# Later head pairs of a sink-and-window attention: two score blocks merged into 128 columns before the softmax, one transpose per head and block, and a triangle mask that parts them again

## The chip, the cores and the metric

The kernel runs on one core of one Trainium2 chip. The metric is device time in microseconds (us) of one execution; the kernel before takes 735.0 us as the median of three runs (734.63 to 736.55). The five engines of the core each work through their own instruction queue in order: PE (matrix multiply, with its weight loads shown apart as PEld), DVE (VectorE), ACT (ScalarE), POOL (GpSimd) and SP (which here only issues transfers). They meet through semaphores.

## The reference

The input has 4 batches, 8 heads, 768 positions and head width 64. Each query sees the first 4 keys (the sinks) and the 128 keys that end with its own position. The attention output then goes through a two-layer network of widths 512, 2048 and 512.

```
scores = scale * np.matmul(q, k.transpose(0, 1, 3, 2))
rel = pos[:, None] - pos[None, :]
keep = (pos[None, :] < n_sink) | ((rel >= 0) & (rel < window))     # n_sink = 4, window = 128
scores = np.where(keep, scores, -1e9)
a = softmax(scores); x = matmul(a, v)       # then per token, over all heads:
h = x @ w_in;  g = h * np.tanh(softplus(h));  out = g @ w_out
```

With a window of 128, a query at row r of a 128-row block sees of its own block the columns c <= r, and of the block before it the columns c > r. Of any column number, it sees one of the two.

## The kernel before, in words

**Tiling.** Work is cut into 12 chunks of 256 tokens (T = 256, two blocks of P = 128 rows; `TB = 2`). Each batch gives three chunks, c3 = 0, 1, 2. A chunk needs four head pairs of attention (`pair`, line 364) and eight steps of the two-layer network (`step`, line 468). The four chunks with c3 = 0 come first; their pairs are the "first" ones (16 pairs). The other eight chunks have the "later" pairs (32 pairs), and only these are touched by the change. The network steps of chunks 3 to 10 are "wide": the first layer uses one 512-column and one 256-column product per weight tile (lines 493 and 494), and DVE adds the halves (line 503).

**A later pair.** A query block needs three groups of key columns: the 128 keys of the older block, 32 sink columns (SK = 32), and the 128 keys of its own block. They lie side by side in `ks`, 288 columns in all (W2). For each of the two blocks and each of the two heads:

- PE makes 288 scores per query into a PSUM tile `st` (line 399).
- DVE adds the mask `m2`, scales, and finds the row's extreme in one pass (line 407, from `st` into `p2`).
- ACT takes the exponential with the row sum (line 410). Two short operations give the reciprocal (lines 413 to 415).
- ACT or DVE multiplies the row by it (lines 420 and 421).
- PE transposes two squares of 128 columns, the older and the own one (line 431), into a PSUM tile `pt`; ACT or DVE copies `pt` to `pth` in SBUF (line 435, by the helper at lines 256 and 259).

Then, once per pair, the 32 sink columns of both blocks and heads are gathered in `psk` (line 439), transposed together (line 440) and copied to `sks`. `out` (line 446) multiplies `pth` by the values (line 449, twelve products) and adds the sink part (line 453, four). The result is split into a high and a low part for the network (lines 457 and 458).

**Order of the work.** A planner (`Plan.solve`, line 123) simulates the engines with fixed costs for every task and gives each engine a fixed order. Each task has a rank (pairs run some nine to eleven steps ahead of the network steps that need them, `att_rank`, line 585) and one or several ways, that is engines which can do it with their planned costs; the planner takes whichever can start first, ties by rank. Tasks on POOL, and those DVE tasks that are marked `shared`, are planned one after the other and never at once. Buffers have a fixed number of places (`TAGS`, line 233): four PSUM places named `att` for scores, transposes and attention outputs, two `p2`, one `pth`. Where the plan leaves PE without work for more than 250 ns, `emit` (line 590) puts in filler products on zeros (line 622).

The costs that the planner uses for what the change touches:

```
def dve_t(n, fast=False): return ((n / 2 if fast else n) + 66) / 0.96      # ns
def pool_t(n): return 149 + 2.1 * n
a = add(r + OTP, {PE: (109 * (2 if cols[0] is None else 4), tr)}, norm, [p2], [pt])
```

**Masks.** `constants` (line 780) builds the masks once at the start on DVE. `body` (line 814) tests whether the window is at most 129 and sinks at most 32; if so the fast form runs, else a general one.

Of the kernel before, what the change touches and what calls it, by code (L numbers as in the profile page):

```python
# [12 lines left out]
F32 = mybir.dt.float32  # L13
BF16 = mybir.dt.bfloat16
F32R = mybir.dt.float32r
I32 = mybir.dt.int32
U32 = mybir.dt.uint32
AF = mybir.ActivationFunctionType
ALU = mybir.AluOpType
# [4 lines left out]
P = 128  # L24
NBLK = S // P
SK = 32
PITCH = P + SK
# [4 lines left out]
TB = 2  # L32
T = TB * P
NCH = NBLK // TB
BIG = 3.0e38
# [7 lines left out]
LAG = {PE: {PE: 0, ACT: 200, DVE: 200}, ACT: {PE: 270, ACT: 143, DVE: 142, POOL: 170}, DVE: {PE: 200, ACT: 120, DVE: 127, POOL: 155},  # L43
       POOL: {PE: 203, ACT: 75, DVE: 80, POOL: 102}, SP: {}}
W2 = 2 * P + SK
PEN_C, PEN_S, PEN_N, PEN_J = 200, 0, 0, 0
OTP, OVP = 1.2, 1
WA, WB, WO = 1.5, -5, 1.5
# [18 lines left out]
def dve_t(n, fast=False):  # L67
    return ((n / 2 if fast else n) + 66) / 0.96
# [161 lines left out]
class Fast(Base):  # L230
# [16 lines left out]

    def setup(self):
        c = self.c
        self.m0, self.m1, self.m2 = c.m0, c.m1, c.m2  # L250

    def copy_ways(self, n, dst, src, psum=False, engines=(ACT, DVE), scale=None):
        nc = self.nc
# [110 lines left out]
    def pair(self, b, c3, pr, rank, x, x_done):  # L364


        nc, add = self.nc, self.plan.add
        first = c3 == 0
        (ks, qh, vt, ldk, ldv), vr, vdeps = self.operands(b, c3, pr, rank - 3)
        pth = Buf("pth", [P, 2, 2 * T])  # L370
        if not first:
            ssk, sks = Buf("att", [P, P]), Buf("sks", [P, P])
        p2 = Buf("p2", [P, TB, 2, W2])
        last, norms = [], []
        for i in range(TB):
            r = rank + i
            nm, sm, rc = Buf("nm", [P, 2]), Buf("sm", [P, 2]), Buf("rc", [P, 2])
            if not first:
                n, mask, c0 = W2, self.m2, i * PITCH
            elif i == 0:  # L380
                n, mask, c0 = P, self.m0, 0
            else:
                n, mask, c0 = 2 * P, self.m1, 0
            st = [Buf("att", [P, n]) for _ in range(2)]

            def mov(rows, n=n, c0=c0):
                if n == 2 * P:
                    return ks.t[rows, 0:2 * PITCH].rearrange("p (a c) -> p a c", c=PITCH)[:, :, 0:P]
                return ks.t[rows, c0:c0 + n]

            def qk(st=st, mov=mov, i=i, c0=c0, n=n):
                cols = slice(i * P, (i + 1) * P)
                for e in range(2):
                    rows = slice(e * D, (e + 1) * D)
                    if first:
                        yield nc.tensor.matmul(st[e].t, qh.t[rows, cols], mov(rows), start=True, stop=True)  # L396
                    else:
                        for n_, part in enumerate(qh):
                            yield nc.tensor.matmul(st[e].t, part.t[:, e, cols], ks[e].t[:, c0:c0 + n], start=n_ == 0, stop=n_ == 1)  # L399
            cost = 2 * (n / 1.2 + 106) + 100 if first else pe_t(*[n] * 4)  # L400
            s = add(r, {PE: (cost, qk)}, ldk, [ks, qh] if first else [*ks, *qh], st)
            ex = []
            for e in range(2):
                new = ([p2] if i == 0 else []) + [nm, sm] if e == 0 else []
                old = [z for z in (p2, nm, sm) if z not in new]
                pv = lambda e=e, n=n, i=i: p2.t[:, i, e, 0:n]
                a = add(r + .03 + .01 * e, {DVE: (dve_t(n) + 8, lambda st=st, pv=pv, nm=nm, e=e, mask=mask, n=n: nc.vector.tensor_tensor_reduce(  # L407
                    out=pv(), in0=st[e].t[:, 0:n], in1=mask, scale=-0.125, scalar=BIG, op0=ALU.add, op1=ALU.min, accum_out=nm.t[:, e:e + 1]))},
                    [s], [st[e]] + old, new)
                a = add(r + .05 + .01 * e, {ACT: (act_t(n, ptr=2), lambda pv=pv, nm=nm, sm=sm, e=e: nc.scalar.activation(  # L410
                    pv(), pv(), AF.Exp, bias=nm.t[:, e:e + 1], scale=-1.0, accum_out=sm.t[:, e:e + 1]))}, [a], [p2, nm, sm])
                ex.append(a)
            a = add(r + .07, {ACT: (act_t(2), lambda rc=rc, sm=sm: nc.scalar.activation(rc.t, sm.t, AF.Copy, bias=1e-9), 0, PEN_N),
                              DVE: (72, lambda rc=rc, sm=sm: nc.vector.tensor_scalar(rc.t, sm.t, 1e-9, None, ALU.add))}, ex, [sm], [rc])
            a = add(r + .08, {DVE: (84, lambda rc=rc: nc.vector.reciprocal(rc.t, rc.t))}, [a], [rc])
            norm = []
            for e in range(2):
                row = lambda e=e, n=n, i=i: p2.t[:, i, e, 0:n]
                norm.append(add(r + .09 + .01 * e, {
                    DVE: shared((dve_t(n, True) + 80, lambda row=row, rc=rc, e=e: nc.vector.tensor_scalar(row(), row(), rc.t[:, e:e + 1], None, ALU.mult))),  # L420
                    ACT: (act_t(n, ptr=1), lambda row=row, rc=rc, e=e: nc.scalar.activation(row(), row(), AF.Copy, scale=rc.t[:, e:e + 1]), 0, PEN_N),  # L421
                }, [a], [p2, rc]))
            norms += norm
            pt = Buf("att", [P, 2, T])
            cols = (0, PITCH) if not first else ((None, 0) if i == 0 else (0, P))

            def tr(pt=pt, cols=cols, i=i):
                for e in range(2):
                    for x in range(2):
                        if cols[x] is not None:  # L430
                            yield nc.tensor.transpose(pt.t[:, e, x * P:(x + 1) * P], p2.t[:, i, e, cols[x]:cols[x] + P], self.ident)  # L431
            a = add(r + OTP, {PE: (109 * (2 if cols[0] is None else 4), tr)}, norm, [p2], [pt])
            lo = P if cols[0] is None else 0
            dst = slice(i * T + lo, (i + 1) * T)
            last.append(add(r + OTP + .05, self.copy_ways(2 * (T - lo), lambda dst=dst: pth.t[:, :, dst], lambda pt=pt, lo=lo: pt.t[:, :, lo:], True),
                            [a], [pt] + ([] if i == 0 else [pth]), [pth] if i == 0 else []))
        if not first:
            psk = Buf("psk", [P, 2 * TB, SK])
            a = add(rank + 1.11, self.copy_ways(P, lambda: psk.t, lambda: p2.t.rearrange("p i e c -> p (i e) c")[:, :, P:PITCH]), norms, [p2], [psk])
            a = add(rank + OTP + 1.02, {PE: (109, lambda: nc.tensor.transpose(ssk.t, psk.t.rearrange("p a c -> p (a c)"), self.ident))}, [a], [psk], [ssk])  # L440
            last.append(add(rank + OTP + 1.09, self.copy_ways(P, lambda: sks.t, lambda: ssk.t, True), [a], [ssk], [sks]))
        r = rank + TB + OVP
        o = Buf("att", [P, T])
        jobs = self.jobs(first)

        def out():
            for n_, (j, c0, c1, o0, o1) in enumerate(jobs):
                for e in range(2):
                    yield nc.tensor.matmul(o.t[e * D:(e + 1) * D, o0:o1], vt.t[:, e, j, :], pth.t[:, e, c0:c1],  # L449
                                           start=n_ == 0, stop=first and n_ == len(jobs) - 1)  # L450
            if not first:
                for i in range(TB):
                    yield nc.tensor.matmul(o.t[:, i * P:(i + 1) * P], vr.t[:, i, :], sks.t, start=False, stop=i == TB - 1)  # L453
        cost = sum(c1 - c0 for _, c0, c1, _, _ in jobs) / .6 + 200 + (0 if first else T / .6 + 50)
        a = add(r + .05, {PE: (cost, out)}, last + ldv + vdeps, [pth, vt] + ([] if first else [vr, sks]), [o])
        h = x[pr]
        a = add(r + .15, self.copy_ways(T, lambda: h.t[:, 0, :], lambda: o.t, True), [a], [o], [h])
        c = add(r + .17, self.sub_ways(T, lambda: h.t[:, 1, :], lambda: o.t, lambda: f32(h.t[:, 0, :]), (DVE,)), [a], [o, h])
        x_done += [a, c]
# [320 lines left out]
def constants(nc, top, tmp, lim):  # L780
# [14 lines left out]
    nc.vector.tensor_scalar(ahead, rel, 0.0, 1.0e6, ALU.is_lt, ALU.mult)  # L795
    nc.vector.tensor_tensor(rel, rel, ahead, ALU.max)
    c.done = nc.vector.tensor_copy(col, col_i)
    c.m0, c.m1, c.m2 = t([P, P], F32, "m0"), t([P, 2 * P], F32, "m1"), t([P, W2], F32, "m2")

    def masks():  # L800
        nsink, window = lim[:, 0:1], lim[:, 1:2]
# [1 line left out]
        drop(col, col, nsink)  # L803
        drop(c.m1[:, P:], rel[:, P:], window)
        nc.vector.tensor_tensor(c.m0, c.m1[:, P:], col, ALU.max)
        drop(c.m2[:, 0:P], rel[:, 0:P], window)
        nc.vector.tensor_tensor(c.m1[:, 0:P], c.m2[:, 0:P], col, ALU.max)
        nc.vector.tensor_copy(c.m2[:, P:PITCH], col[:, 0:SK])
        nc.vector.tensor_copy(c.m2[:, PITCH:], c.m1[:, P:])
    c.masks = masks  # L810
    return c

# [1 line left out]
def body(tc, q, k, v, vs, w_in, w_out, limits, out):  # L814
    nc = tc.nc
    with ExitStack() as ctx:
# [17 lines left out]
        with ExitStack() as c2:  # L834
# [14 lines left out]
            nsink_f, window_f = lim[:, 0:1], lim[:, 1:2]  # L849
            nc.vector.tensor_scalar(ok, nsink_f, float(SK), None, ALU.is_le)  # L850
            nc.vector.scalar_tensor_tensor(ok, window_f, 1.0, ok, ALU.is_ge, ALU.mult)
            nc.vector.scalar_tensor_tensor(flag, window_f, P + 1.0, ok, ALU.is_le, ALU.mult)
            c.masks()
        banded = nc.values_load(flag[0:1, 0:1], min_val=0, max_val=1)
        with tc.If(banded > 0) as cmp:
# [43 lines left out]
```

## Time and profile before

| what | number |
|---|---|
| median of three runs | 735.0 us (734.63 to 736.55) |
| span of the profiled execution, first to last instruction | 732.8 us |
| what lies around that span, if the execution was like the median | 2.2 us |
| PE busy | 717.3 us, 98% |
| DVE busy | 543.9 us, 74% |
| ACT busy | 569.8 us, 78% |
| POOL busy | 134.0 us, 18% |
| later pairs: first score product to last sink product | 194.8 to 668.2 us |

The profiled execution's own time is known by its span alone. Busy shares are unions of overlapping instructions. PE's products are pipelined: a product of 128 columns is listed with some 270 ns, but the next one begins long before it ends, so what a product costs PE is the distance from its start to the start of the next. A line of the timeline gives the start, the duration of the merged instructions, the engine, the line of the kernel, the operation, the tiles as out<-in, the shape and the count; in brackets stands the idle time before it and what ended it. A line of the groups gives the summed busy time, the mean of one instruction in ns, and the idle time before.

### The profile page before, as it was taken

The numbers are of one execution on the slowest core, as the hardware profiler recorded it, in microseconds if no ns is written. First come the engines' busy times: TensorE is split into PE (matmuls) and PEld (weight loads), VectorE is DVE, ScalarE is ACT, GpSimd is POOL, SyncE is SP. The second block draws the span as 40 slices with busy tenths as digits, with TensorE's granted clock in tenths as the row PEclk, the third lists the DMA queues.
The fourth block names the chain that finished last, engine by engine and source line by source line (L and its number), as shares of the span: only waits on it lengthen the run. The fifth ranks groups of instructions, "written<-read, shape, count | busy, mean of one in ns | idle before, by whom it ended". The sixth has DMA issues, their size and how long they took to land.

```text
span 732.8 us, 12975 instructions
## 1 busy us (share of the span) xinstructions
PE 717.3 (98%) x4468; PEld 605.3 (83%) x4468; DVE 543.9 (74%) x1419; ACT 569.8 (78%) x1288; POOL 134.0 (18%) x109
## 2 busy tenths in 40 slices
PE   6999999999999999999999999999999999999996
PEld 4667889888888888888888888888888888888995
DVE  5999999996778877768877667777777867664432
ACT  5999989777977788787788878787787788775653
POOL 0232231201120222121012121130132223100000
PEclk9999999999999999999999999999999999999999
DMA  6555433423353323323233323223313311100000
GB/s 212 163 172 166 139 103 133 124 86 90 103 138 93 82 75 89 81 74 98 65 92 93 79 65 102 72 64 111 87 45 95 109 31 34 49 17 2 30 1 33
DMA packets 48987, 64.12 MB, mean 87 GB/s; under 512 B 4880, under 2 KB 41744, under 8 KB 48912
## 3 DMA queue, kind: packets, MB, share of 16 engines
q1 hardware_dynamic: 48480, 61.62, 29.0%
q10 hardware_dynamic: 432, 1.57, 0.6%
q8 instruction: 37, 0.61, 0.4%
q14 instruction: 38, 0.31, 0.1%
HBM read 56.89 MB, written 6.29 MB: 86 GB/s over the span
## 4 chain that ended last, share of the span: by engine, by line
PE 90%; DVE 4%; ACT 4%; DMA 1%; issue 1%; SPq 0%; ACTq 0%; DVEq 0%
PE acc L527 35%; PE hp L493 16%; PE hp L497 10%; PE hp L494 8%; PE att L449 5%; PE att L399 4%; PE att L431 4%; PE att L453 3%; PE att L497 2%; ACT p L410 1%; PE att L396 1%; DMA qh<-q_p 1%; ACT p L421 1%; DVE p L407 1%; ACT w L256 1%; DVE w L305 1%
## 5 line engine op out<-in xcount | busy, mean ns | idle before, releaser
L527 PE MATMUL acc<-w,gh 128*128 128x512 f32 x768 | 198.4, 396 | 0.2 <-ACT gh L256 0.2
L493 PE MATMUL hp<-w,w 128*128 128x512 f32 x512 | 192.1, 409 | 0.0
L527 PEld LDWEIGHTS acc<-w,gh 128*128 128x128 f32 x768 | 136.1, 188 | 26.3 <-ACT gh L256 0.8
L494 PE MATMUL hp<-w,w 128*128 128x256 f32 x512 | 143.3, 280 | 0.0
L503 DVE TENSOR_REDUCE n<-hp 128x256 f32<-128x512 f32 x128 | 87.8, 687 | 30.5 <-PE hp L494 29.6
L493 PEld LDWEIGHTS hp<-w,w 128*128 128x128 f32 x512 | 96.3, 188 | 17.1 <-issue 0.2
L527 PE MATMUL acc<-w,gl 128*128 128x512 f32 x384 | 108.3, 390 | 0.0
L410 ACT ACTIVATE p<-p,nm 128x288 f32<-128x288 f32 (+1 forms) x192 | 95.3, 499 | 3.6 <-DVE nm L407 3.5
L494 PEld LDWEIGHTS hp<-w,w 128*128 128x128 f32 x512 | 96.8, 189 | 1.5
L407 DVE CUSTOM_DVE_ANT_0 p<-att,m 128x288 f32<-128x288 f32 (+1 forms) x192 | 74.6, 419 | 25.2 <-PE att L399 20.2
L508 ACT ACTIVATE u<-u,bias 128x512 f32<-128x512 f32 x96 | 69.0, 720 | 29.8 <-DVE u L507 29.8
L497 PE MATMUL hp<-w,w 128*128 128x256 f32 x672 | 89.6, 285 | 0.2 <-DVE n L511 0.2
L497 PEld LDWEIGHTS hp<-w,w 128*128 128x128 f32 x672 | 84.9, 191 | 3.9 <-issue 0.5
L527 PEld LDWEIGHTS acc<-w,gl 128*128 128x128 f32 x384 | 71.9, 188 | 14.1
L506 ACT ACTIVATE u<-n 128x512 f32<-128x512 f32 x64 | 40.5, 632 | 54.1 <-DVE n L503 54.1
L267 POOL TENSOR_TENSOR gl<-n,gh 128x512 fp32r<-128x512 f32 x32 | 41.4, 1293 | 202.6 <-ACT gh L256 173.1
L256 ACT ACTIVATE gh<-n 128x512 fp32r<-128x512 f32 x93 | 58.3, 626 | 20.4 <-DVE n L511 20.3
L507 DVE TENSOR_SCALAR u<-u 128x512 f32<-128x512 f32 x96 | 44.7, 466 | 38.2 <-ACT u L506 37.6
L509 ACT ACTIVATE u<-u,bias 128x512 f32<-128x512 f32 x96 | 68.9, 718 | 1.7
L511 DVE SCALAR_TENSOR_TENSOR n<-u,n 128x512 f32<-128x512 f32 x64 | 44.1, 690 | 35.1 <-ACT u L510 34.9
L510 ACT ACTIVATE u<-u 128x512 f32<-128x512 f32 x96 | 60.1, 627 | 1.8
L269 DVE TENSOR_TENSOR gl<-n,gh 128x512 fp32r<-128x512 f32 x64 | 48.2, 754 | 15.4 <-PE acc L527 12.2
(85 smaller groups left out, 1063.3 us busy)
## 6 DMA issues: line engine op xcount, KB each, us to landing
raw<-k_p SPq DMA_DIRECT2D x64, 224.0 KB, 3.5
w<-q_p SPq DMA_DIRECT2D x64, 128.0 KB, 3.2
raw<-w_out SPq DMA_DIRECT2D x15, 512.0 KB, 4.0
raw<-w_in SPq DMA_DIRECT2D x14, 512.0 KB, 3.5
y<-u SPq DMA_DIRECT2D x24, 256.0 KB, 2.0
vt<-v_b SPq DMA_DIRECT2D x32, 192.0 KB, 2.5
vsr<-v_s SPq DMA_DIRECT2D x32, 128.0 KB, 2.3
ks<-k_p SPq DMA_DIRECT2D x16, 144.0 KB, 3.4
```

Source lines behind the costliest of these rows:

```text
L256: ways[ACT] = act_t(n, psum), lambda: nc.scalar.activation(dst(), src(), AF.Copy, scale=scale or 1.0)
L269: way = dve_t(n), lambda: nc.vector.tensor_tensor(dst(), a(), b(), ALU.subtract)
L407: a = add(r + .03 + .01 * e, {DVE: (dve_t(n) + 8, lambda st=st, pv=pv, nm=nm, e=e, mask=mask, n=n: nc.vector.tensor_tensor_reduce(out=pv() ...
L410: a = add(r + .05 + .01 * e, {ACT: (act_t(n, ptr=2), lambda pv=pv, nm=nm, sm=sm, e=e: nc.scalar.activation(pv(), pv(), AF.Exp, bias=nm.t[: ...
L493: yield nc.tensor.matmul(hp.t, wih[f].t[:, fs], xt, start=kt == 0, stop=False)
L494: yield nc.tensor.matmul(hp.t[:, 0, :], wil[f].t[:, fs], xt[:, 0, :], start=False, stop=kt == KT - 1)
L497: yield nc.tensor.matmul(hp.t[:, y, :], w_.t[:, fs], xt[:, z, :], start=kt == 0 and n_ == 0, stop=kt == KT - 1 and n_ == 2)
L503: hs.append(add(r + .3 + .1 * y, {DVE: (dve_t(2 * T), lambda y=y, hp=hp: nc.vector.tensor_reduce(m.t[:, y, :], hp.t.rearrange("p z t -> p ...
L508: a = add(r + .52, {ACT: (act_t(N, ptr=1), lambda: nc.scalar.activation(u.t, u.t, AF.Square, bias=self.one))}, [a], [u])
L509: a = add(r + .53, {ACT: (act_t(N, ptr=1), lambda: nc.scalar.activation(u.t, u.t, AF.Ln, bias=self.half, scale=0.5))}, [a], [u])
L510: a = add(r + .54, {ACT: (act_t(N), lambda: nc.scalar.activation(u.t, u.t, AF.Exp, scale=-1.0))}, [a], [u])
L527: yield nc.tensor.matmul(acc[t].t, g_.t[:, y, ts_], w_.t, start=new and n_ == 0, stop=done)
```

## The change

- **Scores** are made as before, 288 columns. Then DVE overwrites, in PSUM, the own-block columns c > r of `st` by the older block's (`copy_predicated` with an integer triangle mask `older`), once per head and block.
- **Softmax** reads the 32 sink columns and the 128 merged ones: 160 columns (WM) in the mask-and-extreme pass, the exponential and the scaling. The mask is `mm`.
- **Transposes:** one square per head and block. The two transpose tasks of a pair (one per block, four squares each) become one task with four squares, after all four scalings, into one `pt`.
- **Parting them again:** `pt` is copied whole to the "older" half of `pth` (ACT or DVE); DVE multiplies `pt` by a triangle of ones and zeros (`newer`) into the "own" half; POOL or DVE subtracts the own half from the whole. Before, there were two copies of 512 columns per pair; now there are one copy, one product and one subtraction of 512 columns each.
- `psk` takes columns 0 to 31 of `p2`. The products of `out` stay as they are.
- `p2` is 256 columns wide per block and head instead of 288. `constants` makes `mm`, `older` and `newer` in place of `m2`. The test for the fast form asks for a window of at most 128 (it is 128).

```diff
 W2 = 2 * P + SK
+WM = SK + P
...
-                n, mask, c0 = W2, self.m2, i * PITCH
+                n, mask, c0 = W2, self.mm, i * PITCH
...
-            ex = []
+            ex, a0, merged = [], 0, [s, s]
+            if not first:
+                n, a0 = WM, P
+                merged = [add(r + .02 + .01 * e, {DVE: (dve_t(P), lambda z=st[e]: nc.vector.copy_predicated(z.t[:, PITCH:], self.c.older, z.t[:, 0:P]))},
+                              [s], [st[e]]) for e in range(2)]
...
-                    out=pv(), in0=st[e].t[:, 0:n], in1=mask, scale=-0.125, scalar=BIG, op0=ALU.add, op1=ALU.min, accum_out=nm.t[:, e:e + 1]))},
-                    [s], [st[e]] + old, new)
+                    out=pv(), in0=st[e].t[:, a0:a0 + n], in1=mask, scale=-0.125, scalar=BIG, op0=ALU.add, op1=ALU.min, accum_out=nm.t[:, e:e + 1]))},
+                    [merged[e]], [st[e]] + old, new)
...
             norms += norm
+            if not first:
+                continue
             pt = Buf("att", [P, 2, T])
-            cols = (0, PITCH) if not first else ((None, 0) if i == 0 else (0, P))
+            cols = (None, 0) if i == 0 else (0, P)
...
         if not first:
+            pt = Buf("att", [P, 2, TB, P])
+
+            def tr():
+                for i in range(TB):
+                    for e in range(2):
+                        yield nc.tensor.transpose(pt.t[:, e, i, :], p2.t[:, i, e, SK:WM], self.ident)
+            r = rank + 1
+            a = add(r + OTP, {PE: (109 * 4, tr)}, norms, [p2], [pt])
+            part = lambda x: pth.t.rearrange("p e (i x c) -> p x (e i) c", i=TB, x=2)[:, x]
+            whole = lambda: pt.t.rearrange("p e i c -> p (e i) c")
+            b = add(r + OTP + .03, self.copy_ways(4 * P, lambda: part(0), whole, True), [a], [pt], [pth])
+            c = add(r + OTP + .05, {DVE: (dve_t(4 * P), lambda: nc.vector.tensor_tensor(
+                part(1), whole(), self.c.newer[:, None, :].to_broadcast([P, 2 * TB, P]), ALU.mult))}, [a], [pt, pth])
+            last.append(add(r + OTP + .07, self.sub_ways(4 * P, lambda: part(0), lambda: part(0), lambda: part(1)), [b, c], [pth]))
...
-        drop(c.m2[:, 0:P], rel[:, 0:P], window)
-        nc.vector.tensor_tensor(c.m1[:, 0:P], c.m2[:, 0:P], col, ALU.max)
-        nc.vector.tensor_copy(c.m2[:, P:PITCH], col[:, 0:SK])
-        nc.vector.tensor_copy(c.m2[:, PITCH:], c.m1[:, P:])
+        drop(c.m1[:, 0:P], rel[:, 0:P], window)
+        nc.vector.tensor_tensor(c.mm[:, SK:], c.m1[:, 0:P], c.m1[:, P:], ALU.max)
+        nc.vector.tensor_tensor(c.m1[:, 0:P], c.m1[:, 0:P], col, ALU.max)
+        nc.vector.tensor_copy(c.mm[:, 0:SK], col[:, 0:SK])
+        nc.vector.tensor_scalar(c.older, rel_i[:, P:], 0, None, ALU.is_lt)
+        nc.vector.tensor_scalar(c.newer, rel_i[:, P:], 0, None, ALU.is_le)
```

More of the change, by code (lines that the diff above doesn't have):

```diff
@@ L249, in setup @@
         c = self.c
-        self.m0, self.m1, self.m2 = c.m0, c.m1, c.m2
+        self.m0, self.m1, self.mm = c.m0, c.m1, c.mm
     def copy_ways(self, n, dst, src, psum=False, engines=(ACT, DVE), scale=None):
@@ L372, in pair @@
             ssk, sks = Buf("att", [P, P]), Buf("sks", [P, P])
-        p2 = Buf("p2", [P, TB, 2, W2])
+        p2 = Buf("p2", [P, TB, 2, 2 * P])
         last, norms = [], []
@@ L406, in pair @@
                 pv = lambda e=e, n=n, i=i: p2.t[:, i, e, 0:n]
-                a = add(r + .03 + .01 * e, {DVE: (dve_t(n) + 8, lambda st=st, pv=pv, nm=nm, e=e, mask=mask, n=n: nc.vector.tensor_tensor_reduce(
-                    out=pv(), in0=st[e].t[:, 0:n], in1=mask, scale=-0.125, scalar=BIG, op0=ALU.add, op1=ALU.min, accum_out=nm.t[:, e:e + 1]))},
-                    [s], [st[e]] + old, new)
+                a = add(r + .03 + .01 * e, {DVE: (dve_t(n) + 8, lambda st=st, pv=pv, nm=nm, e=e, mask=mask, n=n, a0=a0: nc.vector.tensor_tensor_reduce(
+                    out=pv(), in0=st[e].t[:, a0:a0 + n], in1=mask, scale=-0.125, scalar=BIG, op0=ALU.add, op1=ALU.min, accum_out=nm.t[:, e:e + 1]))},
+                    [merged[e]], [st[e]] + old, new)
                 a = add(r + .05 + .01 * e, {ACT: (act_t(n, ptr=2), lambda pv=pv, nm=nm, sm=sm, e=e: nc.scalar.activation(
@@ L437, in pair @@
         if not first:
+            pt = Buf("att", [P, 2, TB, P])
[11 more added lines that the diff above has]
+            last.append(add(r + OTP + .07, self.sub_ways(4 * P, lambda: part(0), lambda: part(0), lambda: part(1)), [b, c], [pth]))
+        if not first:
             psk = Buf("psk", [P, 2 * TB, SK])
-            a = add(rank + 1.11, self.copy_ways(P, lambda: psk.t, lambda: p2.t.rearrange("p i e c -> p (i e) c")[:, :, P:PITCH]), norms, [p2], [psk])
+            a = add(rank + 1.11, self.copy_ways(P, lambda: psk.t, lambda: p2.t.rearrange("p i e c -> p (i e) c")[:, :, 0:SK]), norms, [p2], [psk])
             a = add(rank + OTP + 1.02, {PE: (109, lambda: nc.tensor.transpose(ssk.t, psk.t.rearrange("p a c -> p (a c)"), self.ident))}, [a], [psk], [ssk])
@@ L797, in constants @@
     c.done = nc.vector.tensor_copy(col, col_i)
-    c.m0, c.m1, c.m2 = t([P, P], F32, "m0"), t([P, 2 * P], F32, "m1"), t([P, W2], F32, "m2")
+    c.m0, c.m1, c.mm = t([P, P], F32, "m0"), t([P, 2 * P], F32, "m1"), t([P, WM], F32, "mm")
+    c.older, c.newer = t([P, P], I32, "older"), t([P, P], F32, "newer")
     def masks():
@@ L851, in body @@
             nc.vector.scalar_tensor_tensor(ok, window_f, 1.0, ok, ALU.is_ge, ALU.mult)
-            nc.vector.scalar_tensor_tensor(flag, window_f, P + 1.0, ok, ALU.is_le, ALU.mult)
+            nc.vector.scalar_tensor_tensor(flag, window_f, float(P), ok, ALU.is_le, ALU.mult)
             c.masks()
```

## The prediction

> **What bounds the kernel now.** I read the page first (span, the busy slices of PE with its granted clock, the chain of work that ended last), then the busy times of the stretch in which the later pairs run, then the source view of the transposes and the timeline of PE around one group of them.
>
> ```profile
> span 732.8 us, 12975 instructions
> ...
> PE   6999999999999999999999999999999999999996
> ...
> PEclk9999999999999999999999999999999999999999
> ...
> PE 90%; DVE 4%; ACT 4%; DMA 1%; issue 1%; SPq 0%; ACTq 0%; DVEq 0%
> ```
>
> PE is busy in every slice after the first, at full granted clock, and 90% of the chain is PE's own work. Now the stretch from the first score product of a later pair to the last sink product:
>
> ```profile
> core 0: us, PE busy (x) PEld busy (x) DVE busy (x) ACT busy (x) POOL busy (x), PEclk, DMA share, GB/s
> 195.00:668.00 473.00, 472.81 (x2851) 399.07 (x2850) 345.64 (x892) 371.10 (x832) 93.13 (x72) 1.00 0.27 76
> ```
>
> PE is busy for 472.81 of 473.00 us. VectorE has 127 us to spare, ScalarE 102 us. So here a microsecond of PE work that goes away is a microsecond of time, as long as nothing that PE waits for gets late. The stretch holds all 32 later pairs, so a pair has 473/32 = 14.8 us, in which VectorE works 10.8 us and ScalarE 11.6 us.
>
> **What the change removes on PE.** Busy PE says nothing of how tightly its products are packed, and a product's listed duration is that of a pipeline. So the price is read from starts.
>
> ```profile
> L431 PE MATMUL att<-ident,p x352: 270/272/332, 13.3 to 663.0; 128*128 128x128 f32 x176
> ```
>
> ```profile
> 411.03 0.60 PE L431 MATMUL att<-ident,p 128*128 128x128 f32 x4
> 411.38 0.47 PE L493 MATMUL hp<-w,w 128*128 128x512 f32 x1
> 411.70 0.28 PE L494 MATMUL hp<-w,w 128*128 128x256 f32 x1
> 411.81 0.40 PE L493 MATMUL hp<-w,w 128*128 128x512 f32 x1
> 412.05 0.28 PE L494 MATMUL hp<-w,w 128*128 128x256 f32 x1
> 412.16 0.27 PE L440 MATMUL att<-ident,psk 128*128 128x128 f32 x1
> 412.19 0.47 PE L493 MATMUL hp<-w,w 128*128 128x512 f32 x1
> 412.50 0.28 PE L494 MATMUL hp<-w,w 128*128 128x256 f32 x1
> 412.62 0.40 PE L493 MATMUL hp<-w,w 128*128 128x512 f32 x1
> ```
>
> A 512-column product at line 493 normally hands over after 0.24 us (411.81 to 412.05). With the four transposes in front, the way from the first of them to the end of that product's turn is 411.03 to 411.70 = 0.67 us. The four cost 0.67 - 0.24 = 0.43 us. The single transpose of the sink columns gives the same price: 412.16 to 412.50 is 0.34 us, less 0.24 is 0.10 us. So one transpose is worth 0.10 to 0.11 us of PE time, the shadow on the product behind it included.
>
> The 352 transposes are 96 of the first pairs (16 pairs with six) and 256 of the later ones (32 with eight). The change leaves four per later pair, in one group: 128 transposes go, 32 x 0.43 = 13.8 us. The 288-column score products, the twelve products with the values and the sink part stay, and no transfer is added or moved. Against the profiled span: 732.8 - 13.8 = 719.0 us; with the 2.2 us by which the median of the runs stands above this span, 721.2 us.
>
> [...]
>
> **What it adds on VectorE and ScalarE.** Rows of the shapes that change, each at two widths, and the nearest for what is new:
>
> ```profile
> L410 ACT ACTIVATE p<-p,nm 128x288 f32<-128x288 f32 x128 | 66.7, 523 | 0.4 <-DVE nm L407 0.4
> ...
> L407 DVE CUSTOM_DVE_ANT_0 p<-att,m 128x288 f32<-128x288 f32 x128 | 53.3, 453 | 20.4 <-PE att L399 20.2
> ...
> L267 POOL TENSOR_TENSOR gl<-n,gh 128x512 fp32r<-128x512 f32 x32 | 41.4, 1293 | 202.6 <-ACT gh L256 173.1 <-PE hp L494 16.2 <-PE att L399 11.2
> ...
> L256 ACT ACTIVATE pth<-att 128x512 f32<-128x512 f32 x66 | 38.9, 589 | 8.5 <-PE att L431 8.3 <-PE att L449 0.2
> ...
> L420 DVE TENSOR_SCALAR p<-p,rc 128x288 f32<-128x288 f32 x79 | 28.8, 391 | 1.7
> ...
> L421 ACT ACTIVATE p<-p,rc 128x288 f32<-128x288 f32 x49 | 25.0, 527 | 3.1 <-DVE rc L415 2.6
> ...
> L511 DVE SCALAR_TENSOR_TENSOR n<-u,hp 128x512 f32<-128x512 f32 x28 | 19.1, 682 | 2.5 <-ACT u L510 2.5
> ...
> L407 DVE DVE_READ_ACCUMULATOR2_ANT nm<- 128x1 f32 x192 | 16.0, 84 | 0.0
> ...
> L410 ACT ACTIVATE p<-p,nm 128x128 f32<-128x128 f32 x32 | 12.6, 397 | 2.5 <-DVE nm L407 2.4
> ...
> L259 DVE COPY pth<-att 128x512 f32<-128x512 f32 x14 | 9.6, 684 | 0.3 <-PE att L431 0.3
> ...
> L407 DVE CUSTOM_DVE_ANT_0 p<-att,m 128x128 f32<-128x128 f32 x32 | 8.6, 284 | 2.0 <-PE att L396 1.8 <-PE att L431 0.2
> L309 DVE TENSOR_TENSOR w<-w,w 128x512 f32<-128x512 f32 x11 | 7.6, 688 | 0.1
> ...
> L421 ACT ACTIVATE p<-p,rc 128x128 f32<-128x128 f32 x18 | 6.8, 393 | 0.0
> ...
> L420 DVE TENSOR_SCALAR p<-p,rc 128x128 f32<-128x128 f32 x14 | 4.7, 347 | 0.1
> ...
> L259 DVE COPY sks<-att 128x128 f32<-128x128 f32 x6 | 1.7, 288 | 0.9 <-PE att L440 0.8
> ```
>
> By a straight line between the 128- and 288-column rows, 160 columns cost 318 ns in the mask pass (453 - 0.8 x 169), 422 in the exponential, 420 in ScalarE's scaling and 356 in VectorE's. Per later pair (four rows of each kind):
> - VectorE saves 4 x 135 = 0.54 us in the mask pass, and 79/128 of four scalings at 35 ns each, 0.09. ScalarE saves 4 x 101 = 0.40 in the exponential and 49/128 of four scalings at 107, 0.16.
> - One of two copies to `pth` goes: 0.49 us from ScalarE (66 of 80 such copies) and 0.12 from VectorE.
> - The product with the triangle reads 512 columns of PSUM with one mask from SBUF, as line 511 does from `hp`: 0.68 us on VectorE.
> - The subtraction of 512 columns is SBUF only: 1.29 us on POOL (line 267) or 0.69 on VectorE (line 309). Its strided halves are not in the trace; 128 columns stand together, so I take the plain rows.
> - The four predicated copies are the unknown: no row shows VectorE writing to PSUM or a predicated copy. An instruction that is added can't give time back; below lies the smallest row, 84 ns (the accumulator read at line 407), above lie 128 columns at the price of 512, 0.69 us, should mask, source and kept data go through one after another. The nearest are the 128-column copy out of PSUM, 288 ns, and the 128-column mask pass, which has the same two inputs, 284. I take 288: 4 x 0.288 = 1.15 us.
>
> Sum for VectorE: + 1.15 + 0.68 - 0.54 - 0.09 - 0.12 = + 1.1 us, or + 1.8 with the subtraction; for ScalarE - 1.05. A pair would then have 14.35 us, with VectorE busy 11.9 to 12.6 (83 to 88%) and ScalarE 10.5 (74%). The planner may move copies and scalings to ScalarE. At the upper price of the predicated copy VectorE comes to 14.2 us, 99%; at the lower, to 11.1. All of this is hidden behind PE: it costs nothing as long as PE's inputs are in time; with VectorE full, what exceeds a pair's 14.35 us would be paid.
>
> **Who waits longer.** The chain of a pair grows by two predicated copies ahead of the mask passes and by product and subtraction behind the copy to `pth`. How much room is there?
>
> ```profile
> 399.99 1.38 DVE L507 TENSOR_SCALAR u<-u 128x512 f32<-128x512 f32 x1
> ...
> 401.49 0.65 DVE L420 TENSOR_SCALAR p<-p,rc 128x288 f32<-128x288 f32 x2
> ```
>
> ```profile
> 411.50 0.62 ACT L256 ACTIVATE gh<-n 128x512 fp32r<-128x512 f32 x1
> ```
>
> ```profile
> 416.36 0.87 PE L449 MATMUL att<-pth,vt 128*64 128x256 f32 x8
> ```
>
> The scalings of this pair's second block (line 420, 401.49, two of them) ended at 402.14, and its transposes began at 411.03: the wait for all four scalings costs nothing with 8.9 us to go. From the transposes' start to the products with the values (416.36) there are 5.3 us; the new way needs about 0.6 for four transposes, 0.7 for the product, 1.3 for the subtraction on POOL and some 0.5 of handovers, 3.1 us. What stands behind the transposes on PE is line 493 of the network step. On VectorE the predicated copies wait for the scores just as the mask passes did, and the product waits for the transposes; behind either stand lines 503, 507 and 511 of the network. The subtraction holds up POOL's other subtractions, `gl` among them. `pth` has one place and is now taken after the second block instead of the first; of the four `att` places a pair takes seven in turn instead of eight, two of them some 0.3 us longer.
>
> Tighter is the network's own chain. `gh` ended at 411.50 + 0.62 = 412.12, and its products start here:
>
> ```profile
> 412.97 2.00 PE L527 MATMUL acc<-w,gh 128*128 128x512 f32 x8
> ```
>
> That is 0.85 us of room in a step, and VectorE stands three times in the chain to `gh` (lines 503, 507, 511). [...]
>
> ```profile
> 399.94 1.15 POOL L267 TENSOR_TENSOR w<-raw,w 64x448 fp32r<-64x448 f32 x1
> ```
>
> Line 507 took 1.38 us from 399.99, while POOL's two-input subtraction ran until 401.09; line 309 above, with two inputs of as many columns, takes 0.69. So line 507 was held until POOL was done. [...]
>
> The plan has room for most of this elsewhere; I allow 1 us in all for such delays: 721.2 + 1 = 722.2 us, forecast 722.
>
> **At the start** two more mask instructions (nine instead of seven, at 0.2 to 0.3 us each) run on VectorE:
>
> ```profile
> 7.61 0.23 DVE L809 COPY m<-m 128x128 f32<-128x128 f32 x1
> ...
> 9.60 0.29 DVE L407 CUSTOM_DVE_ANT_0 p<-att,m 128x128 f32<-128x128 f32 x1 [1.77 <-PE att L396]
> ```
>
> The masks end at 7.84 us and the first mask pass starts at 9.60, having idled 1.77 us for PE: 0.6 us more costs nothing; without that cover it would cost 0.6.
>
> **The rivals.**
> - *Half the gain is lost to waits.* The chain to `gh` is late by more than its 0.85 us in some steps, 0.2 us per pair on average: 721.2 + 32 x 0.2 = 727.6. For it: VectorE rises from 73% to 83 to 88% with copies that arrive in bursts. Against: PE lost 0.19 us in 473 with VectorE at 73%.
> - [...] The subtraction runs on POOL while line 507 is due; that is held for up to 1.29 us, and the product of 0.68 us stands in front of it as well: 1.97 - 0.85 = 1.12 us late at `gh`. If that happens in every second pair, 16 x 1.12 = 17.9 us: 721.2 + 17.9 = 739. From 0.44 us per pair on, nothing is left of the gain. Against: the plan never puts POOL and a `shared` operation at one time, and can give the subtraction to VectorE.
> - *The transposes cost only their streaming.* If the 0.11 us hide weight loads that other products would then bear, 128 columns at half of the 0.12 us that 256 take (412.50 to 412.62) are worth 0.06 us: 128 x 0.06 = 7.7, 735.0 - 7.7 = 727.3. Against: the two prices in the timeline agree.
> - *The planner gives the time back.* The longer chain leaves holes in its plan, and `emit` fills them:
>
> ```profile
> L622 PE MATMUL acc<-zero x102: 259/259/394, 10.9 to 207.7; 128*128 128x224 bf16 x102
> ```
>
>   The fillers stop at 207.7 us, when the later pairs have hardly begun; 0.43 us of them per pair would eat the gain: 735. That the fast form isn't taken can be left out: the window is 128 and passes the new test.
>
> **How the numbers follow.** Forecast 0.72 (own range 720 to 725), half lost 0.12 (727.6), streaming only 0.03 (727.3), given back 0.05 (735), slower 0.08 (739). The likeliest gives 722. The range starts at 719.5: no delay (721.2), 0.4 for the runs' spread below their median, and 1.3 of the tenth of the chain (73 us) that isn't PE's and that another order may close. It ends at 729, which takes in half the gain lost and the transposes' lower price; together 0.87. A difference of 0.3% is 2.2 us, which is about what a measurement of this kernel can tell from none: faster 0.87, same 0.05, slower 0.08.
>
> **What would show it.** Right: 224 transposes at line 431 and its successor together, 0.43 us per group; PE busy within 0.5 us of the stretch, which is some 459 us long; VectorE at 83 to 88% there; predicated copies near 0.29 us. Wrong: idle time on PE that ends with `gh`, `pth` or line 503; fillers after 208 us; predicated copies near 0.7 us; line 507 often at 1.4 us. A gain near 7 us with PE packed would say that the price of a transpose was wrong.

## The result, and the profile after

The changed kernel takes 721.89 us (median of four runs, 721.41 to 722.02) against 735.28 us for the kernel before on the same chip. The ratio is 0.9816, with a 95% interval of 0.9802 to 0.9829: 13.4 us, or 1.8%, faster. Its profiled execution has a span of 719.9 us and a time of 721.78 us, so 1.9 us lie around the span (2.2 were assumed).

From the page of the changed kernel, the span, PE's busy time and busy slices, and the chain that ended last:

```profile
span 719.9 us, 12890 instructions
...
PE 704.4 (98%) x4338; PEld 592.3 (82%) x4338; DVE 565.1 (78%) x1546; ACT 557.8 (77%) x1310; POOL 149.8 (21%) x122
...
PE   6999999999999999999999999999999999999996
...
PE 88%; DVE 6%; ACT 4%; DMA 1%; issue 1%; SPq 0%; ACTq 0%; DVEq 0%
```

PE's busy time fell by 12.9 us (717.3 to 704.4), nearly all of the gain. Its busy slices stayed as they were, and its share of the chain went from 90% to 88%. The last product of the later pairs now starts at 655.8 us instead of 668.2. The windows view of their stretch has the columns of the prediction's header (PE, PEld, VectorE, ScalarE and POOL, each with busy us and count, then PE's clock, DMA share and GB/s):

```profile
195.00:655.00 460.00, 459.54 (x2720) 385.69 (x2720) 367.21 (x1018) 358.32 (x853) 107.58 (x84) 1.00 0.28 78
```

PE is busy for 459.54 of 460.00 us. VectorE went from 73% to 80%, ScalarE from 78.5% to 78%, POOL from 20% to 23%. The one group of transposes that a pair has left, in the timeline of PE:

```profile
403.86 0.60 PE L450 MATMUL att<-ident,p 128*128 128x128 f32 x4
404.22 0.48 PE L515 MATMUL hp<-w,w 128*128 128x512 f32 x1
404.53 0.28 PE L516 MATMUL hp<-w,w 128*128 128x256 f32 x1
```

It costs 404.53 - 403.86 = 0.67 us less the usual 0.24, so 0.43 us as before; there is one of these per pair instead of two. The groups of the changed and added instructions (line, engine, operation, tiles, shapes and count; busy us and mean ns; idle before):

```profile
L549 PE MATMUL acc<-w,gh 128*128 128x512 f32 x768 | 197.0, 396 | 0.5 <-ACT gh L257 0.5
...
L415 ACT ACTIVATE p<-p,nm 128x160 f32<-128x160 f32 x128 | 53.3, 417 | 0.8 <-DVE nm L412 0.4
...
L412 DVE CUSTOM_DVE_ANT_0 p<-att,mm 128x160 f32<-128x160 f32 x128 | 36.1, 320 | 0.2
L406 DVE COPY_PREDICATED att<-older,att 128x128 f32<-128x128 int32 x128 | 33.5, 293 | 22.9 <-PE att L400 22.6
...
L426 ACT ACTIVATE p<-p,rc 128x160 f32<-128x160 f32 x73 | 28.1, 420 | 4.9 <-DVE rc L420 4.4
...
L268 POOL TENSOR_TENSOR pth<-pth 128x512 f32<-128x512 f32 x19 | 24.6, 1296 | 84.5 <-DVE pth L456 84.5
...
L270 DVE TENSOR_TENSOR pth<-pth 128x512 f32<-128x512 f32 x13 | 9.9, 759 | 0.2
```

The predicated copy takes 293 ns, where I had taken 288. The mask pass at 160 columns takes 320 (318), the exponential 417 (422), ScalarE's scaling 420 (420), VectorE's 384 (356), the triangle product 682 (682), the subtraction 1296 on POOL (1290) and 759 on VectorE (690). The planner sent 19 of the 32 subtractions to POOL and 13 to VectorE, and moved scalings to ScalarE (73 instead of 49). PE's products with `gh` waited 0.5 us in all. Fillers stop earlier than before, at 81 us:

```profile
L644 PE MATMUL acc<-zero x100: 259/259/394, 10.7 to 81.1; 128*128 128x224 bf16 x100
```

### The profile page after: what moved, and what is told of

Its sections match the earlier page's. It is cut to its first block, busy times and chain, and to the rows that moved or that the text cites. A ratio compares the mean times of both kernels' runs of the same rounds, so it can differ in the third digit from the quotient of the medians.

```text
span 719.9 us, 12890 instructions
## 1 busy us (share of the span) xinstructions
PE 704.4 (98%) x4338; PEld 592.3 (82%) x4338; DVE 565.1 (78%) x1546; ACT 557.8 (77%) x1310; POOL 149.8 (21%) x122
## 4 chain that ended last, share of the span: by engine, by line
PE 88%; DVE 6%; ACT 4%; DMA 1%; issue 1%; SPq 0%; ACTq 0%; DVEq 0%
PE acc L549 36%; PE hp L515 16%; PE hp L519 11%; PE hp L516 8%; PE att L471 5%; PE att L400 4%; PE att L475 3%; PE att L450 2%; PE att L519 2%; ACT p L415 1%; PE att L397 1%; DMA qh<-q_p 1%; DVE w L270 1%; DVE p L412 1%; ACT p L426 1%; PE att L438 1%
## 5 line engine op out<-in xcount | busy, mean ns | idle before, releaser
L515 PE MATMUL hp<-w,w 128*128 128x512 f32 x512 | 189.0, 405 | 0.0
L549 PE MATMUL acc<-w,gl 128*128 128x512 f32 x384 | 109.8, 391 | 0.0
L525 DVE TENSOR_REDUCE n<-hp 128x256 f32<-128x512 f32 x128 | 87.3, 685 | 13.8 <-PE hp L516 12.6
L415 ACT ACTIVATE p<-p,nm 128x160 f32<-128x160 f32 (+1 forms) x192 | 82.0, 429 | 3.9 <-DVE nm L412 3.4
L268 POOL TENSOR_TENSOR gl<-n,gh 128x512 fp32r<-128x512 f32 x36 | 46.6, 1294 | 136.4 <-ACT gh L257 99.0
L270 DVE TENSOR_TENSOR gl<-n,gh 128x512 fp32r<-128x512 f32 x60 | 44.7, 746 | 15.3 <-PE acc L549 12.2
L309 POOL TENSOR_TENSOR w<-w,w 128x512 f32<-128x512 f32 x21 | 29.4, 1406 | 114.0 <-DVE w L306 106.6
```

The costliest lines, as they stand in the source:

```text
L268: ways[POOL] = pool_t(n), lambda: nc.gpsimd.tensor_tensor(dst(), a(), b(), ALU.subtract)
L270: way = dve_t(n), lambda: nc.vector.tensor_tensor(dst(), a(), b(), ALU.subtract)
L515: yield nc.tensor.matmul(hp.t, wih[f].t[:, fs], xt, start=kt == 0, stop=False)
L525: hs.append(add(r + .3 + .1 * y, {DVE: (dve_t(2 * T), lambda y=y, hp=hp: nc.vector.tensor_reduce(m.t[:, y, :], hp.t.rearrange("p z t -> p ...
L549: yield nc.tensor.matmul(acc[t].t, g_.t[:, y, ts_], w_.t, start=new and n_ == 0, stop=done)
```

## The experiments

Theory: PE sets the time in the stretch, a group of four transposes is worth 0.43 us of it, and the work added on VectorE and POOL is hidden. The rivals were that the gain came from elsewhere or that a transpose costs only its streaming, that the additions do cost waits, and that POOL's subtraction and VectorE's queue pace PE. The runs lie on several chips, on which the kernel before took 734.88 to 735.28 us, and each ratio is to the kernel before on the same chip; so a difference in us between two runs of less than about 1 us says little.

### The four transposes put back (e1_four_back)

```diff
-                for i in range(TB):
+                for i in range(2 * TB):
                     for e in range(2):
-                        yield nc.tensor.transpose(pt.t[:, e, i, :], p2.t[:, i, e, SK:WM], self.ident)
+                        yield nc.tensor.transpose(pt.t[:, e, i % TB, :], p2.t[:, i % TB, e, SK:WM], self.ident)
```

> The changed kernel with the four transposes of each later pair issued twice into the same place; the plan and the order of all other work are untouched. Theory (the gain is 0.43 us of PE time per group of four): 721.9 + 32 x 0.43 = 735.7 us, which is the kernel before, and PE stays packed. Rival (a transpose costs only its streaming, 0.06 us, and the rest of the gain came from lighter work on VectorE and ScalarE): 721.9 + 128 x 0.06 = 729.6 us.

Measured: 735.42 us, ratio 1.0006 (0.9997 to 1.0016) to the kernel before. That is 13.53 us over the changed kernel, or 0.42 us per pair (14.0 us and 0.44 by the difference of the two ratios). PE's timeline around one group, and the stretch:

```profile
409.80 1.03 PE L450 MATMUL att<-ident,p 128*128 128x128 f32 x8
410.59 0.47 PE L515 MATMUL hp<-w,w 128*128 128x512 f32 x1
410.90 0.28 PE L516 MATMUL hp<-w,w 128*128 128x256 f32 x1
```

```profile
195.00:668.00 473.00, 472.57 (x2841) 399.07 (x2841) 372.66 (x1018) 358.57 (x853) 106.82 (x84) 1.00 0.27 76
```

Eight transposes take 410.90 - 409.80 = 1.10 us against 0.67 for four: 0.43 us for four, and PE stays packed. So the whole gain is these 128 transposes. The streaming rival, with 7.7 us, is out.

### No merging and no parting (e4_no_parting)

```diff
-                merged = [add(r + .02 + .01 * e, {DVE: (dve_t(P), ... copy_predicated ...)}, [s], [st[e]]) for e in range(2)]
...
-            c = add(r + OTP + .05, {DVE: (dve_t(4 * P), ... tensor_tensor(part(1), whole(), newer, ALU.mult))}, [a], [pt, pth])
-            last.append(add(r + OTP + .07, self.sub_ways(4 * P, part(0), part(0), part(1)), [b, c], [pth]))
+            last += [b, add(r + OTP + .05, self.copy_ways(4 * P, lambda: part(1), whole, True), [a], [pt, pth])]
```

> The changed kernel without the predicated copies, and with the triangle product and the subtraction replaced by a second plain copy of the transposed square; the older block's scores are therefore left out and the two halves are alike, so the result lacks that part. PE's work is the same; VectorE loses 1.2 + 0.7 us and up to 0.7 more per pair. Theory (all that the change adds on VectorE and POOL is hidden): 721 to 722 us. Rival (the additions cost PE waits, which is why the stretch of the later pairs shrank by 12.6 us and not by 13.8): 720 us or less.

Measured: 721.43 us, ratio 0.9816 (0.9799 to 0.9832), 0.5 us below the changed kernel and within the spread of both.

```profile
195.00:655.00 460.00, 459.45 (x2723) 385.08 (x2722) 327.37 (x867) 353.95 (x852) 99.74 (x78) 1.00 0.28 78
```

VectorE is busy for 327 us of the same window instead of 367, and the time is the same. The 40 us of VectorE work that merging and parting put in are hidden: 0.5 us by the medians and nothing by the ratios, 0.9816 for both kernels, is too little to be told from none. This run also made one more plain copy of 512 columns per pair, on ScalarE or VectorE, and the planner ordered it anew.

### How far the cover goes: the predicated copies two, three and six times

```diff
-                merged = [add(r + .02 + .01 * e, {DVE: (dve_t(P), lambda z=st[e]: nc.vector.copy_predicated(z.t[:, PITCH:], self.c.older, z.t[:, 0:P]))},
+                merged = [add(r + .02 + .01 * e, {DVE: (dve_t(P), lambda z=st[e]: [nc.vector.copy_predicated(z.t[:, PITCH:], self.c.older, z.t[:, 0:P]) for _ in range(3)])},
```

(six and two in the other runs)

> The changed kernel with every predicated copy issued three times, the plan untouched. In the trace two copies and the start of the mask pass behind them lie 0.235 us apart each, so eight more per pair put 1.9 us on VectorE: 11.5 + 1.9 = 13.4 us of a pair's 14.4 (93%). Theory (PE covers it): 722 to 724 us. Rival (VectorE's queue paces PE, as the chain to gh has only 0.85 us of room and each of the 64 blocks is now 0.94 us later): half of that reaching PE is 64 x 0.47 = 30 us, 752 us.

> The same with six times: 20 more copies per pair, 4.7 us, so VectorE would need 16.2 us of a pair's 14.4. Theory (the cover ends where VectorE is full): 721.9 + 32 x (16.2 - 14.4) = 780 us, PE idle behind VectorE. Rival (waits on VectorE start far earlier than fullness): well over 780 us, in proportion to the 20 copies, up to 721.9 + 32 x 4.7 = 872 us.

Measured: 762.91 us with three (ratio 1.0384, 1.0367 to 1.0401) and 907.35 us with six (1.2362, 1.2338 to 1.2387). My theory was wrong for both, and six copies went beyond the rival's upper end of 872 us as well. With three, VectorE isn't full, yet PE waits. The stretch of that kernel, and who waited for whom (total us, times, longest):

```profile
195.00:690.00 495.00, 466.59 (x2684) 381.74 (x2683) 425.15 (x1267) 354.88 (x848) 106.41 (x83) 1.00 0.26 73
```

```profile
PEld acc L549 <- ACT gh L257: 36.8, 41, 2.4
...
PE acc L549 <- ACT gh L257: 25.7, 25, 2.2
```

VectorE is busy for 86% of the window (425.15 of 495). The wait is for `gh`. How the copies lead to it is in the timelines of VectorE, ScalarE and PE in one step of that kernel:

```profile
360.39 1.80 DVE L406 COPY_PREDICATED att<-older,att 128x128 f32<-128x128 int32 x6
362.10 0.32 DVE L412 CUSTOM_DVE_ANT_0 p<-att,mm 128x160 f32<-128x160 f32 x1
```

```profile
362.46 0.43 ACT L415 ACTIVATE p<-p,nm 128x160 f32<-128x160 f32 x1 [1.32 <-DVE nm L412]
...
363.30 0.71 ACT L530 ACTIVATE u<-u,bias 128x512 f32<-128x512 f32 x1
...
367.02 0.63 ACT L257 ACTIVATE gh<-n 128x512 fp32r<-128x512 f32 x1 [1.21 <-DVE n L533]
```

```profile
367.70 0.50 PE L549 MATMUL acc<-w,gh 128*128 128x512 f32 x1 [2.08 <-ACT gh L257]
```

The mask passes begin 1.71 us after the first copy. ScalarE's queue holds the exponentials of the mask passes (362.46) in front of the network's line 530, and the lines up to `gh` come after that. ScalarE stands idle for 1.32 us until the first mask pass is done, everything behind it moves by as much, `gh` ends at 367.65, and PE has waited 2.08 us for it. That is more than 1.32, because the step had come late to ScalarE already: its line 528 began 4.43 us before the score products in front of PE's wait, and 5.73 us before them in the changed kernel. The same step of the changed kernel, on VectorE, ScalarE and PE:

```profile
341.40 0.48 DVE L406 COPY_PREDICATED att<-older,att 128x128 f32<-128x128 int32 x2
341.80 0.32 DVE L412 CUSTOM_DVE_ANT_0 p<-att,mm 128x160 f32<-128x160 f32 x1
```

```profile
342.16 0.43 ACT L415 ACTIVATE p<-p,nm 128x160 f32<-128x160 f32 x1
...
343.00 0.71 ACT L530 ACTIVATE u<-u,bias 128x512 f32<-128x512 f32 x1
...
346.72 0.63 ACT L257 ACTIVATE gh<-n 128x512 fp32r<-128x512 f32 x1 [1.21 <-DVE n L533]
```

```profile
347.78 0.64 PE L549 MATMUL acc<-w,gh 128*128 128x512 f32 x2
```

There the mask passes begin 0.40 us after the first copy, the exponentials wait for nothing, and `gh` ends at 347.35, 0.43 us before PE takes it. From the exponential to `gh` it is 4.56 us in both kernels. How long ScalarE's exponentials waited for mask passes in the whole run, with three copies and in the changed kernel:

```profile
ACT p L415 <- DVE nm L412: 51.5, 51, 2.4
```

```profile
ACT p L415 <- DVE nm L412: 3.4, 5, 2.4
```

By the median of all 64 blocks the mask passes begin 1.72 us after the first copy, and 0.47 us in the changed kernel. So three copies make a block 1.25 us late, of which 41.0/64 = 0.64 us were paid. The price is lateness in ScalarE's fixed order, long before VectorE is full. Line 533 on VectorE, which `gh` needs, stands behind the copies too in many steps; how the 41 us divide between the two ways isn't shown.

> The changed kernel with every predicated copy issued twice, the plan untouched. With three, copies into one place followed each other 0.30 us apart, a block's mask passes began 1.72 us after the first copy instead of 0.47, so 1.25 us later, and the kernel paid 41.0/64 = 0.64 us per block. With two they should be some 0.65 us later. Theory (each block has about 0.6 us of room before gh holds PE, and all beyond it is paid): 722 to 726 us. Rival (half of any delay is paid): 721.9 + 64 x 0.33 = 743 us.

Measured: 733.65 us, ratio 0.9977 (0.9966 to 0.9987): 11.8 us over the changed kernel, 0.18 per block.

```profile
PEld acc L549 <- ACT gh L257: 11.5, 19, 1.7
...
PE acc L549 <- ACT gh L257: 6.1, 11, 1.5
```

```profile
195.00:668.00 473.00, 466.30 (x2731) 386.53 (x2730) 393.52 (x1147) 359.57 (x854) 107.98 (x84) 1.00 0.28 76
```

By the median the mask passes begin 1.06 us after the first copy, so a block is 0.59 us late, and 0.41 of it is absorbed. Neither expectation holds: there is no one threshold of 0.6 us, nor a fixed share. PE's weight loads waited for `gh` 19 times here and 41 times with three copies, in the kernel's 96 steps. Pairing each `gh` of the changed kernel with its first product, over the 60 steps between 205 and 640 us, suggests why:

```
end of gh to its first product: least 0.05, lower quartile 0.64, median 0.98, most 2.43 us
```

The room differs from step to step, so each further delay reaches more steps. That explains the direction and not the size: summed over these steps, a delay of 0.59 us exceeds the room by 4.1 us and one of 1.25 us by 22.8, while 11.8 and 41.0 us were paid. A step that begins late, like the one above, has less room than it had in the changed kernel; that this makes up the rest isn't shown.

### The same three copies, with the plan told (e8_x3_planned)

```diff
-... {DVE: (dve_t(P), lambda z=st[e]: [ ... for _ in range(3)])}
+... {DVE: (860, lambda z=st[e]: [ ... for _ in range(3)])}
```

> Every predicated copy three times, as before, but the plan is told what three cost (860 ns instead of 202). VectorE has the same work or nearly so. Theory (what was paid is lateness against a plan that did not know, not a full VectorE): the plan moves flexible copies and scalings to ScalarE and puts the chain to gh ahead; 722 to 735 us. Rival (VectorE is full at 14.0 of a pair's 14.4 us): 755 us or more.

Measured: 722.84 us, ratio 0.9831 (0.9815 to 0.9848). Of the 41.0 us only 1.0 is left, though VectorE does all the extra copies. Window, group of the products with `gh`, and ScalarE's wait for mask passes:

```profile
195.00:655.00 460.00, 458.86 (x2713) 385.28 (x2713) 396.80 (x1173) 370.76 (x907) 161.00 (x128) 1.00 0.28 78
```

```profile
L549 PE MATMUL acc<-w,gh 128*128 128x512 f32 x768 | 196.9, 396 | 0.0
```

```profile
ACT p L415 <- DVE nm L412: 18.3, 22, 2.5
```

VectorE is as full as with the plan not told (86%), POOL took 161 us of the window instead of 108, and the products with `gh` never waited. ScalarE waited 18.3 us for mask passes instead of 51.5. Line 533 stood straight behind all copies and both mask passes of a block in 35 of the 64 wide steps with the plan not told, and in 2 here. Telling the price did two things, though: it changed the orders, and it took other work off VectorE, which was busy for 396.80 us of this stretch and 425.15 of the longer one with the plan not told. The run with two copies tells the two apart: there VectorE was busy for 393.52 us of its stretch, about as long as here, and 11.8 us were lost. So the loss was in the main the order, not the amount of VectorE's work.

### The subtraction on one engine (e5_sub_dve, e6_sub_pool)

```diff
-self.sub_ways(4 * P, lambda: part(0), lambda: part(0), lambda: part(1))
+self.sub_ways(4 * P, lambda: part(0), lambda: part(0), lambda: part(1), (DVE,))     # (POOL,) in the other
```

> The changed kernel with the subtraction on VectorE alone (in the changed kernel 19 of 32 run on POOL). Theory (the subtraction is hidden on either engine): 721 to 723 us. [...]

> The changed kernel with the subtraction on POOL alone. Theory (hidden on either engine): 721 to 723 us. [...]

Measured: 723.89 us on VectorE alone (ratio 0.9845, 0.9828 to 0.9861) and 723.59 us on POOL alone (0.9837, 0.9821 to 0.9854). Both are 2.0 and 1.7 us above the changed kernel, a little over what I expected. From the waits: the run on VectorE alone, the run on POOL alone, and the changed kernel:

```profile
PEld acc L549 <- ACT gh L257: 4.3, 10, 1.0
```

```profile
PEld acc L549 <- ACT gh L257: 2.5, 5, 0.8
```

```profile
PEld acc L549 <- ACT gh L257: 1.2, 3, 0.6
```

Either bound leaves the planner one choice less. The first edit does one thing more: a subtraction that only VectorE can do loses the mark `shared`, so the plan may put it beside work of POOL. It then took 924 ns in the mean instead of 759, and 13 of the 32 took 0.97 to 1.69 us while POOL's `gl` ran. How the 2.0 us divide isn't shown. The hold of line 507 (now 529) beside POOL's subtraction doesn't pace the kernel: with no subtraction on POOL it was no faster, and with 13 more there it lost 1.7 us, not the 13 x 1.12 = 14.6 that the prediction's 1.12 us late at `gh` would give.

### The next cut on PE (e9_sink_fp32r)

If PE is what counts, its next fp32 products should pay in the same way. Here the sink part is taken with products of rounded operands (fp32r), which the profile lists as two instructions per pair instead of four:

```diff
-            ssk, sks = Buf("att", [P, P]), Buf("sks", [P, P])
+            ssk, sks = Buf("att", [P, P]), Buf("sks", [P, P], F32R)
+            vq = Buf("w", [P, TB, P], F32R)
...
+            vdeps = [add(rank + OTP + .9, self.copy_ways(T, lambda: vq.t, lambda: vr.t), vdeps, [vr], [vq])]
...
-                    yield nc.tensor.matmul(o.t[:, i * P:(i + 1) * P], vr.t[:, i, :], sks.t, start=False, stop=i == TB - 1)
+                    yield nc.tensor.matmul(o.t[:, i * P:(i + 1) * P], vq.t[:, i, :], sks.t, start=False, stop=i == TB - 1)
-        cost = sum(c1 - c0 for _, c0, c1, _, _ in jobs) / .6 + 200 + (0 if first else T / .6 + 50)
...
+        cost = sum(c1 - c0 for _, c0, c1, _, _ in jobs) / .6 + 200 + (0 if first else pe_t(P, P))
...
```

The planner is told the lower cost as well.

> The changed kernel with the sink part's product taken in the rounded one-pass format that the network uses, in place of full fp32: the sink weights are rounded when they are copied out of PSUM, the sink values by one more copy of 256 columns per pair on ScalarE or VectorE. This keeps less precision in the sink part. In the changed kernel the four sink instructions hold PE 0.47 us (210.21 to 410.68 in the four hundreds of the timeline, that is 410.21 to 410.68) and the product behind them 0.08 longer, 0.55 us per pair; two one-pass products of 128 columns should hold it 0.13 to 0.25. Theory (a microsecond of PE in this stretch is a microsecond of time, again): 721.9 - 32 x 0.36 = 710 us, 708 to 713. Rival (with PE shorter still the chain to gh, or VectorE with the added copy, paces the stretch): less than half of it, 716 us or more.

Measured: 714.36 us, ratio 0.9719 (0.9702 to 0.9735), 7.5 us below the changed kernel: faster than both kernels, with the operands of the sink part rounded. Both expectations missed the size. PE's timeline shows why, first in the changed kernel, then in this one, then this one's stretch:

```profile
410.21 0.71 PE L475 MATMUL att<-sks,vsr 128*128 128x128 f32 x4
410.68 0.48 PE L515 MATMUL hp<-w,w 128*128 128x512 f32 x1
411.00 0.28 PE L516 MATMUL hp<-w,w 128*128 128x256 f32 x1
```

```profile
407.05 0.44 PE L478 MATMUL att<-sks,w 128*128 128x128 f32 x2
407.32 0.45 PE L518 MATMUL hp<-w,w 128*128 128x512 f32 x1
407.61 0.28 PE L519 MATMUL hp<-w,w 128*128 128x256 f32 x1
```

```profile
195.00:650.00 455.00, 454.08 (x2673) 380.21 (x2673) 362.94 (x1028) 360.84 (x869) 123.92 (x97) 1.00 0.28 79
```

From the first sink product to the end of the next product's turn it was 411.00 - 410.21 = 0.79 us and is 407.61 - 407.05 = 0.56: 0.23 us saved per pair, and 32 x 0.23 = 7.4 us. PE is as packed as before (454.08 of 455.00). That a microsecond of PE is one of time held; my estimate of 0.13 (the planner's cost, `pe_t(P, P)`) to 0.25 us for the two products was too low, they take 0.27 up to the next start and 0.05 behind it.

## Why the prediction was right

- **What bounds the kernel, and the price of a transpose.** Right. The step "32 x 0.43 = 13.8 us" measured 13.5 us as time (e1_four_back; 14.0 by the ratios) and 0.43 us per group in the trace.
- **The added work is hidden.** Right: e4_no_parting shows 0.5 us or less, where I had allowed 1 us. The prices per instruction were within some 10%, the unknown predicated copy included. VectorE ended at 80% of the stretch, below the forecast 83 to 88%, and ScalarE at 78% instead of 74%. In part this is the planner moving scalings to ScalarE (24 more, at 384 ns on VectorE some 9 us), which the prediction named as possible but did not count.
- **Where the cover ends.** Here the reasoning was half wrong, without effect on the forecast. The prediction read 0.85 us of room at `gh`, which is near the median of 0.98. But it priced the upper end of the unknown copy as a VectorE at 99%, of which only what exceeds a pair's time would be paid. The runs show that lateness is paid first: four copies per block instead of two, with VectorE at 83% (393.52 of 473), already cost 11.8 us. Two copies into one tile delay a block about as one copy of 0.6 us would. So by an estimate from e7_copies_x2, at that price nearly all of the gain would have gone, unless the plan knew it.
- **Line 507 and POOL.** Line 529 (507 before) took over 1 us, and up to 1.31, in 6 of its 96 runs, against a median of 0.43; each time POOL's new subtraction was running and line 529 ended 0.27 to 0.29 us after it (552.33 to 553.63 us, with POOL's from 552.05 to 553.35), although the plan never puts the two at one time. What holds it isn't shown. But putting all subtractions on POOL cost 1.7 us. The slower rival (739 us) named a real delay and overrated how often it meets a step without room.
- **Filler work and the start.** As forecast: no filler after 81 us, and nothing lost at the start.

That 722 fell on 721.89 is partly luck. The kernel before took 735.28 us in the comparison instead of 735.0, the transposes were worth 13.5 to 14.0 us instead of 13.8, and of the 1 us for waits 0.5 or less was found. These offset each other, and each is smaller than what two runs can tell apart.

## What to carry to other kernels

Where one engine is packed, price a removed instruction by the distance between starts, with the shadow on what follows, and put the same instruction back to test it; busy means and listed durations would both have misled here (a transpose is listed with 0.27 us and was worth 0.11). Work moved to a less busy engine is not free up to that engine's fullness: what it delays in a fixed order counts first (two copies for one cost 11.8 us with VectorE at 83%), so read the room between the last input of the bounding engine and its use, over many steps. And where an order is planned from costs, tell the planner the price of the new work: the same extra copies cost 41.0 us untold and 1.0 us told.

## What the runs showed of the hardware

- A predicated copy of 128 columns within PSUM, with a mask from SBUF, takes 293 ns (the changed kernel, line 406, mean of 128). In the run with three copies, copies into the same tile start 0.32 to 0.33 us apart (e2_copies_x3, 256 of them) and the next copy into another tile 0.205 us after the last; six of them take 1.80 us.
- Two products of rounded operands (fp32r) of 128 columns take 0.27 us from the first to the start of the next product (e9_sink_fp32r, 407.05 to 407.32), where one of 256 columns takes 0.11 us (407.61 to 407.72).
